# One turned tile for R, V and scaled A, and R loaded two tokens a partition, in a chunked RWKV-7 layer with a squared-ReLU feed-forward on one core

## The chip, the core and the metric

The kernel runs on one core of one Trainium2 chip. The metric is the device time of one execution in microseconds, lower is better. Before the change three runs took 263.15, 271.69 and 261.65 us, so the median is 263.15. One more execution, the profiled one, took 262.35 us with a span of 260.7 us between its first and its last instruction.

The engines that appear below: PE (TensorE, matmuls and transposes; PEld is its weight load), DVE (VectorE), ACT (ScalarE), POOL (GpSimd), and SP (SyncE), which only issues DMAs. Each works through its own instructions in their order and waits for others by semaphores.

## What is computed

Inputs are six tensors r, k, v, w, a, b of 4 batches x 8 heads x 768 tokens x 40, and two weights, 320 x 2048 and 2048 x 320. For every batch and head a 40 x 40 state runs over the tokens; then a feed-forward with a squared ReLU follows:

```python
for t in range(S):
    y[:, :, t] = np.einsum('bhd,bhde->bhe', rt, state)
    Sa = np.einsum('bhde,bhe->bhd', state, at)
    state_decay = state * wt[:, :, None, :] - np.einsum('bhd,bhe->bhde', Sa, bt)
    state = state_decay + np.einsum('bhd,bhe->bhde', vt, kt)
...
h = x @ w_in
r = np.maximum(h, 0.0)
g = r * r
return (g @ w_out).astype(np.float32)
```

Here x is y with the heads of a token side by side, 3072 x 320.

## The kernel before

The tokens are cut into 6 chunks of 128, so that there are 24 "batches" m (chunk m // 4, batch element m % 4), each with 8 heads, and 48 steps st (a half batch of four heads each). A batch goes through these stages; every stage has a short name, and the whole program is a list of such names.

- Loads on SP (`load`, line 85): lW, lK, lB, lA, lV, lR, each 128 tokens x 8 heads x 40 floats, 160 bytes a row. K and B share a tile, R and V share one. There are four buffers of each.
- The decay: ln takes the logarithm of w, cs sums it over the tokens by a matmul, xi and gp take exponentials (GI, GP), cx the difference between.
- Scaling and casting into padded tiles (each head's 40 columns padded to 64, so that two heads fill 128): pk makes K*GI and B*GI, pa makes A*GP (line 207), both into the padded tile KBA; cv casts R and V into the padded tile RV (lines 153, 155, 157 by engine).
- Turning (heads' dimensions onto the partitions). TensorE transposes into PSUM (`turned`, line 218) followed by an eviction: kt with kv for K and B in batches 0 to 19, ta with at for A and rm with rv for R and V in batches 0 to 7. DMA transposes on SP for the rest: ka (line 255) turns A from batch 8 on, and K, B and A together in the last four batches; rt (line 231) turns R and V from batch 8 on.
- a (st_a_mm, line 287) multiplies turned K and B with turned A for a step. av0 and av1 evict the two products with a mask on VectorE, or plainly on ScalarE, in which case POOL cuts them with aq0 and aq1. p, m, k1, c, k2, s, x (b_p, b_m, corr, b_c1, b_sn, b_x) solve for the step's corrections in PSUM.
- t and tv turn the corrections; e (st_ex_mm, line 410) multiplies turned R with turned V and with the corrections; ev0, ev1, eq0, eq1 evict and cut as before. z, kb, y, u (st_z, st_kb, st_y, st_u) make the output and the next state.
- xt and xv turn the output for the feed-forward; fr, fa, fb are its first matmuls, ra and rb the ReLU on ScalarE, q the square on POOL or VectorE (line 568), o1 and o2 the second matmuls, ov the eviction and ow the store.
- wt, wd and wo load the weights (POOL issues; wd, line 508, is a copy on SP of one piece of the first weight into the other half of the partitions, and waits for that piece). w are matmuls on ones that do nothing but keep TensorE busy. f and i fill tiles with constants. jk, en, ep, es and fl check a bound on the data, by which a general loop would replace the last steps.

What sets the order is the string ORDER: it lists all names with their batch or step, with the engine after a colon (`:P` POOL, `:D` VectorE, `:A` ScalarE) and the PSUM bank after `@`. The program is emitted in that order, and each engine, and SP with its DMAs, works in it. `pick` holds engine and bank of each name; whether a batch has, say, a `kt` at all is also read from it, as in b_ka.

The transposes that the change touches read as follows before it:

```python
def b_rt(m):
    o = bt[m]
    nc.sync.dma_start_transpose(
        out=o.RVT[:].rearrange("p u j t -> p (u j) t"),
        in_=o.RV[:].rearrange("p u h e -> p (u h e)"))
```

Of the kernel before, what the change touches and what calls it, by code (L numbers as in the profile page):

```python
# [18 lines left out]
def kernel(  # L19
# [62 lines left out]
    def load(key, m):  # L82
        pair, u = SHARED.get(key, (key, 0))
        c, bb = divmod(m, NB)
        nc.sync.dma_start(
            out=natural(pair, m)[:, u],
            in_=nat_srcs[key][bb, :, c * L:(c + 1) * L, :].rearrange("h t e -> t h e"))
# [8 lines left out]
    IDb = gl.tile([128, 128], BF16, name="IDb")  # L96
    MEX = gl.tile([128, 4, L], BF16, name="MEX")
# [10 lines left out]
    def fill(k):  # L108
# [7 lines left out]
        elif k < 16:  # L116
            key, i = (("KBA", k - 5) if k < 9 else ("G", k - 9) if k < 12 else ("RV", k - 12))
# [43 lines left out]
    def home(m):  # L161
        o = bt[m] = Batch()
        o.G, o.KB, o.RV = (pads[key][m % len(pads[key])] for key in ("G", "KBA", "RV"))
        o.RVT, o.YN = RVs[m % 4], YNs[m % 3]
# [41 lines left out]
    def b_pa(m):  # L206
        engine("pa", m).tensor_tensor(out=bt[m].KB[:, 2, :, 0:D], in0=nat.pop(("A", m))[:, 0],  # L207
                                      in1=bt[m].GP[:], op=ALU.mult)

    def b_cv(m):  # L210
        move(pick["cv", m][0], bt[m].RV[:, :, :, 0:D], nat.pop(("RV", m))[:])

    def turned(pad, us=(0, 1), t_=None, **place):
        if t_ is None:
            t_ = ps.tile([128, len(us), PB, L], BF16, name="tt", **place)
        for x, u in enumerate(us):
            for j in range(PB):
                nc.tensor.transpose(
                    out=t_[:, x, j, :], identity=IDb[:],
                    in_=pad[:, u, 2 * j:2 * j + 2, :].rearrange("p a b -> p (a b)"))  # L220
        return t_

    def b_rm(m):
        bt[m].t1 = turned(bt[m].RV, **bank("rm", m))

    def b_rv(m):
        move(pick["rv", m][0], bt[m].RVT[:], bt[m].t1[:])

    def b_rt(m):
        o = bt[m]  # L230
        nc.sync.dma_start_transpose(
            out=o.RVT[:].rearrange("p u j t -> p (u j) t"),
            in_=o.RV[:].rearrange("p u h e -> p (u h e)"))
# [4 lines left out]
    def kbt(m):  # L238
        o = bt[m]
        if not hasattr(o, "KBT"):  # L240
            o.KBT = chp.tile([128, 3, PB, L], BF16, name="KBT", tag="KBT", bufs=4)
        return o.KBT

    def b_kv(m):
        move(pick["kv", m][0], kbt(m)[:, 0:2], bt[m].t2[:])

    def b_ta(m):
        bt[m].t3 = turned(bt[m].KB, us=(2,), **bank("ta", m))

    def b_at(m):  # L250
        move(pick["at", m][0], kbt(m)[:, 2], bt[m].t3[:, 0])

    def b_ka(m):
        o, lo = bt[m], 2 if ("kt", m) in pick else 0
        nc.sync.dma_start_transpose(
            out=kbt(m)[:, lo:3].rearrange("p u j t -> p (u j) t"),
            in_=o.KB[:, lo:3].rearrange("p u h e -> p (u h e)"))
# [22 lines left out]
    def st_a_mm(st):  # L280
# [3 lines left out]
        for u in range(2):  # L284
            for i in range(2):
                for s in range(2):
                    nc.tensor.matmul(out=ca[s][:, i, u, :], lhsT=o.KBT[half(s), u, j0 + i, :],  # L287
                                     rhs=o.KBT[half(s), 2, j0 + i, :], start=(i == 0 and u == 0),
# [32 lines left out]
    def b_p(m):  # L321
# [3 lines left out]
        if c > 0:  # L325
            for j in range(PB):
                nc.tensor.matmul(out=P[:, j, :, 0:D], lhsT=o.KBT[:, 2, j, :],
# [292 lines left out]
    def get_flag():  # L620
# [4 lines left out]
        f.0:D lW.0 f.1:P w.1@f f.14:D f.5:P w.16@0 lW.1 i.1 w.8@s lK.0 w.4@f f.3:D i.0 ln.0 f.2:P  # L625
        f.6:P cs.0@s w.7@f w.2@1 cx.0 ln.1 f.10:P lB.0 cs.1@u xi.0 lA.0 f.20:D w.0@f gp.0 pk.0:D
        kt.0@0 lK.1 xi.1 lB.1 f.8:P f.11:D f.16:P w.14@f pa.0:P ta.0@f at.0:A w.15@s cx.1 w.3@x
        gp.1 lW.2 i.2 f.4:P lA.1 lW.3 kv.0:D a.0@0e a.1@xf lV.0 pk.1:D ln.2 av0.0:D pa.1:D f.15:P
        av1.1:A w.11@f av0.1:A av1.0:A lR.0 cs.2@u f.12:P lV.1 cx.2 ta.1@f kt.1@1 w.13@e xi.2
        aq0.0 at.1:D kv.1:D lR.1 a.2@x1 gp.2 av0.2:D av1.2:D aq1.2 a.3@fu lK.2 w.10@0 aq0.2 aq1.1  # L630
        aq0.1 lB.2 cv.0:A aq1.0 ln.3 av0.3:D f.19:P f.18:P p.0@e m.0:A cs.3@0 lK.3 k1.0 jk.0 xi.3
        av1.3:D w.9@x cv.1:A lA.2 rm.0@u c.0 lB.3 aq0.3 cx.3 aq1.3 f.9:P k2.0 p.1@f lA.3 gw.0:P
        gw.2:D gw.1:P s.0:A t.0@f rv.0:D gc.0@s lW.4 tv.0:D f.7:P m.1:A w.12@e f.17:P pk.2:D k1.1
        lV.2 f.13:P wt.1 e.1@0f ev1.1:D pa.2:P ev0.1:D jk.1 rm.1@x pk.3:P gp.3 lW.5 kt.2@e eq0.1
        rv.1:A ta.2@f lR.2 at.2:A lV.3 kv.2:D e.0@u1 ev0.0:A eq0.0 c.1 eq1.1 a.4@ex k2.1 gw.3:D
        av0.4:A z.1@0 ev1.0:D eq1.0 pa.3:P x.0 gl.0 s.1:A kt.3@u aq0.4 cv.2:P lR.3 kb.1 z.0@s
        av1.4:D kb.0 t.1@f gl.1 u.0 y.0 ta.3@x at.3:D kv.3:A ln.4 tv.1:A a.5@ef av0.5:D av1.5:A
        wt.2 u.1 aq1.4 e.3@s1 ev1.3:A lA.4 aq1.5 ev0.3:A y.1 a.6@fx av0.6:D ln.5 eq1.3 a.7@ef
        av1.6:A cs.4@1 av1.7:D eq0.3 e.2@uf cx.4 aq0.5 lK.4 av0.7:D gp.4 aq0.6 ev0.2:D cs.5@f
        ev1.2:D z.3@u p.2@0 xt.0@x pa.4:P xi.5 rm.2@e aq1.6 wt.4 m.2:A z.2@f lB.4 k1.2 wt.3 aq0.7  # L640
        eq0.2 xi.4 lK.5 eq1.2 c.2 kb.2 wt.9 k2.2 rv.2:A cx.5 cv.3:A ta.4@e lB.5 aq1.7 kb.3 wd.0
        p.3@1 lA.5 wt.0 u.2 y.2 s.2:A at.4:D y.3 wt.7 pk.4:D xv.0:A m.3:A t.2@f rm.3@f tv.2:D k1.3
# [275 lines left out]
```

## Time and profile before

| | |
|---|---|
| three runs, us | 263.15, 271.69, 261.65 |
| profiled execution, us | 262.35 |
| its span, us | 260.7 |
| busy PE | 243.1 (93%) |
| busy DVE | 204.7 (79%) |
| busy ACT | 205.7 (79%) |
| busy POOL | 207.9 (80%) |
| DMA packets, MB | 184470, 38.48 |
| packets under 512 bytes | 180064 |

The page gives the busy time of each engine, its share of the span and the costliest groups of instructions. A group's row has the line, the engine and the operation, what is written and read, the count, the busy time and the mean in nanoseconds, and then how long the engine was idle just before these instructions and what ended that. Matmuls overlap, so that the mean of one (about 220 ns for a transpose) is longer than the distance between two. SP's instructions are DMA issues; a duration of such a row contains waiting for a place in the queue. A window's row has its length, the busy time and count of PE, PEld, DVE, ACT and POOL, then the clock granted to TensorE, the mean busy share of the 16 DMA engines, and GB/s.

### The profile page before, as it was taken

To read this page: it belongs to the slowest core of one execution; us is meant where nothing else is said; L and a number is where in the kernel's file an instruction comes from. 1 tells how busy PE (TensorE), PEld (TensorE's weight loads), DVE (VectorE), ACT (ScalarE), POOL (GpSimd) and SP (SyncE) were. 2 spreads that over 40 slices of the span, in tenths; PEclk is the share of its full clock that TensorE was granted. 3 is DMA by queue.
4 is the path that set the end of the run, shared out by engine and by line. 5 is a ranking of instruction groups with operands and counts; after the bars stand their busy time and mean duration, and the time that the engine had idled before them with its cause. 6 is when DMAs were issued, how large, how long until landed. Compare 5 with 4: busy or idle time off the path is not lost.

```text
span 260.7 us, 9854 instructions
## 1 busy us (share of the span) xinstructions
PE 243.1 (93%) x4020; PEld 201.9 (77%) x4020; DVE 204.7 (79%) x421; ACT 205.7 (79%) x470; POOL 207.9 (80%) x238
## 2 busy tenths in 40 slices
PE   8987887999999999999999988999799998999993
PEld 7876676988788877778868777788778886888872
DVE  2789986899899997989787957787889979965240
ACT  3688995999798888878978878898789777678830
POOL 5597998599998574989698996899889468968640
PEclk9999997999999999999999999999999999999998
DMA  7999998999988999989989999999899985022011
GB/s 125 153 178 167 158 191 159 182 155 173 181 144 143 148 165 170 179 168 181 177 148 177 157 174 172 177 158 192 162 160 189 175 146 101 28 69 78 28 55 60
DMA packets 184470, 38.48 MB, mean 148 GB/s; under 512 B 180064, under 2 KB 183136, under 8 KB 184416
## 3 DMA queue, kind: packets, MB, share of 16 engines
q1 hardware_dynamic: 183072, 35.14, 78.8%
q0 software_dynamic: 1344, 2.62, 6.2%
q8 instruction: 33, 0.54, 0.9%
q14 instruction: 21, 0.17, 0.2%
HBM read 28.84 MB, written 3.93 MB: 126 GB/s over the span
## 4 chain that ended last, share of the span: by engine, by line
PE 24%; POOL 13%; DMA 5%; issue 3%; ACT 2%; DVE 2%; SPq 1%; POOLq 0%; DVEq 0%; ACTq 0%
PE hp L542 7%; DMA NW<-in_w_dram 3%; POOL Gt L568 3%; POOL EX L307 2%; POOL KBAp L202 2%; DMA KBT<-KBAp 2%; POOL x L360 2%; POOL KBAp L207 2%; POOL Cc L361 1%; PE ca L287 1%; PE ex L410 1%; PE P L344 1%; PE uy L456 1%; ACT hs L562 1%; PE op__6251 L577 1%
## 5 line engine op out<-in xcount | busy, mean ns | idle before, releaser
L542 PE MATMUL hp<-XS,WIN 128*128 128x256 bf16 (+3 forms) x720 | 73.1, 255 | 2.4 <-DMA WIN<-in_moe_w_in_dram 1.5
L562 ACT ACTIVATE hs<-hp 128x512 bf16<-128x512 f32 x96 | 55.1, 599 | 15.0 <-PE hp L542 9.4
L542 PEld LDWEIGHTS <-WIN 128*128 128x128 bf16 (+1 forms) x720 | 49.9, 115 | 9.6 <-issue 6.3
L568 POOL TENSOR_TENSOR Gt<-hs 128x1024 bf16<-128x1024 bf16 x24 | 45.9, 1914 | 8.7 <-ACT hs L562 6.2
L302 DVE TENSOR_TENSOR CN<-ca,MEX 128x512 bf16<-128x512 f32 x63 | 41.5, 683 | 7.6 <-PE ca L287 6.9
L577 PEld LDWEIGHTS <-Gt 128*128 128x128 bf16 x384 | 35.6, 98 | 13.2 <-issue 0.9
L302 DVE TENSOR_TENSOR EX<-ex,MEX 128x512 bf16<-128x512 f32 x58 | 38.1, 682 | 1.9 <-PE ex L410 0.9
L307 POOL TENSOR_SCALAR_AFFINE_SELECT EX<-EX 128x512 bf16<-128x512 bf16 x38 | 28.0, 744 | 7.6 <-ACT EX L300 7.1
L307 POOL TENSOR_SCALAR_AFFINE_SELECT CN<-CN 128x512 bf16<-128x512 bf16 x33 | 22.2, 677 | 10.6 <-ACT CN L300 8.4
L300 ACT ACTIVATE EX<-ex 128x512 bf16<-128x512 f32 x38 | 22.0, 599 | 5.7 <-PE ex L410 5.6
L207 POOL TENSOR_TENSOR KBAp<-NA,GP 128x320 bf16<-128x320 f32 x18 | 16.6, 922 | 11.6 <-DMA NA<-in_a_dram 5.7
L365 ACT ACTIVATE jk<-CN 128x1024 bf16<-128x1024 bf16 x24 | 25.4, 1057 | 0.0
L202 POOL TENSOR_TENSOR KBAp<-NKB,GI 128x640 bf16<-128x640 f32 x14 | 22.0, 1572 | 1.3 <-PE ca L287 0.7
L300 ACT ACTIVATE CN<-ca 128x512 bf16<-128x512 f32 x33 | 19.5, 603 | 4.3 <-PE ca L287 4.0
L361 POOL TENSOR_TENSOR Cc<-x,SN 128x320 bf16<-128x320 f32 x24 | 20.3, 846 | 1.9
L456 PE MATMUL uy<-KBAp,EX 128*128 128x40 bf16 x384 | 21.7, 181 | 0.0
L568 DVE TENSOR_TENSOR Gt<-hs 128x1024 bf16<-128x1024 bf16 x24 | 21.4, 897 | 0.2
L360 POOL TENSOR_TENSOR x<-Mc,c 128x320 f32<-128x320 bf16 x24 | 19.9, 829 | 0.2
L287 PE MATMUL ca<-KBT 64*128 64x128 bf16 x384 | 18.1, 217 | 1.6 <-ACT KBT L153 0.6
L173 PE MATMUL cs<-lnW,UTI 128*128 128x320 f32 x48 | 19.1, 481 | 0.3 <-ACT CN L300 0.2
L456 PEld LDWEIGHTS <-EX 128*128 128x128 bf16 x384 | 18.4, 97 | 1.3 <-issue 0.7
L344 PEld LDWEIGHTS <-CN 128*128 128x128 bf16 x384 | 15.0, 96 | 4.8 <-issue 3.0
(150 smaller groups left out, 624.4 us busy)
## 6 DMA issues: line engine op xcount, KB each, us to landing
NW<-in_w_dram SPq DMA_DIRECT2D x24, 160.0 KB, 3.8
NKB<-in_k_dram SPq DMA_DIRECT2D x24, 160.0 KB, 3.8
NKB<-in_b_dram SPq DMA_DIRECT2D x24, 160.0 KB, 3.8
NA<-in_a_dram SPq DMA_DIRECT2D x24, 160.0 KB, 4.0
NRV<-in_v_dram SPq DMA_DIRECT2D x24, 160.0 KB, 3.8
NRV<-in_r_dram SPq DMA_DIRECT2D x24, 160.0 KB, 3.9
out_dram<-osb SPq DMA_DIRECT2D x24, 160.0 KB, 3.0
WOUT<-in_moe_w_out_dram POOLq DMA_DIRECT2D x2, 640.0 KB, 7.2
```

Source lines behind the costliest of these rows:

```text
L202: engine("pk", m).tensor_tensor(out=bt[m].KB[:, 0:2, :, 0:D], in0=nat.pop(("KB", m))[:], op=ALU.mult, in1=bt[m].GI[:].rearrange("p (u h) e ...
L300: nc.scalar.activation(out=out, in_=in_[:], func=ACTF.Copy)
L302: nc.vector.tensor_tensor(out=out, in0=in_[:], op=ALU.mult, in1=MEX[:].rearrange("p (i u) x -> p i u x", u=2))
L307: nc.gpsimd.affine_select(out=t_, in_=t_, pattern=[[0, 2], [0, 2], [1, L]], compare_op=ALU.is_gt, fill=0.0, base=0, channel_multiplier=-1)
L360: nc.gpsimd.tensor_tensor(out=t_[:], in0=part(Mc, m), in1=c1s.pop(m)[:], op=ALU.add)
L361: nc.gpsimd.tensor_tensor(out=part(Cc, m), in0=t_[:], in1=flat(SNs[m % NSN]), op=ALU.subtract)
L365: nc.scalar.activation(out=jk[:], in_=CNs[m, "b"][:].rearrange("p x i s u t -> p (x i s) u t")[:, :, 1, :], func=ACTF.Square, accum_out=AC ...
L456: nc.tensor.matmul(out=uy[:, (2 * i + s) * D:(2 * i + s + 1) * D], lhsT=EXs[st][:, i, s, u, :], rhs=o.KB[:, u, 2 * (j0 + i) + s, 0:D], sta ...
L542: nc.tensor.matmul(out=o.hp[u][:, i], lhsT=inner(g, rows, j), rhs=XSs[o.c][rows, g, o.bs, :], start=(o.begun[u] == 1), stop=(o.begun[u] > ...
L562: nc.scalar.activation(out=o.hs[:, u], func=ACTF.Relu, in_=o.hp[u][:].rearrange("p j a b -> p (j a b)"))
L568: engine("q", n).tensor_tensor(out=o.Gt[:, o.j0:o.j0 + 2 * o.per].rearrange("p j a b -> p (j a b)"), in0=hs, in1=hs, op=ALU.mult)
L577: nc.tensor.matmul(out=ops[n][:], rhs=WOUT[:, j, :], lhsT=Gts[h][:, b_, j, :] if h in SPLIT else Gts[h][:, j, b_, :], start=(j == 0), stop ...
```

## The change

The padded tile KBA becomes KB, and RV becomes RVA: scaled A is written behind R and V. The turned tiles move likewise (KBT has two parts, RVT three), and st_a_mm and b_p read turned A there. From batch 8 on, rt turns R, V and A with one DMA; ka is left for the last four batches alone, where it turns K and B. So there are 16 rt and 4 ka where there were 16 and 16.

In batches 0 to 7 R is loaded "paired": two DMAs of 64 partitions each, one for heads 0 to 3 and one for heads 4 to 7; a partition holds two neighbouring tokens, which lie side by side in memory, 320 bytes. A new name cr casts R from that layout, cv casts V alone there. turn_pairs turns R with four transposes whose results are laid into PSUM so that the even tokens come first; V is turned with a second identity IDp that sorts the tokens in the same way; rv then stores both with a stride of two, which puts the tokens back in their order. Turned A of these batches goes through ta and at as before, into the new place.

The whole of ORDER is new: order, engines and banks. The counts of the names are the same but for cr (8, new), ka (4 for 16) and i (4 for 3, IDp). Of engines: 130 of the masked evictions av and ev are on VectorE for 121 before; pk has 17 on POOL for 14; q has 22 on POOL for 24; gw has 18 on POOL for 16; tv has 18 on VectorE for 21, kv 11 for 13, rv 1 for 3; ov 7 for 10, m 11 for 8, pa 7 for 6, s 9 for 8, xv 13 for 12. Of the 21 fills 10 are on POOL for 16. fl stands before the last three w's instead of behind them.

The diff without ORDER, cut to its core:

```diff
     def load(key, m):
...
+        src, dst = nat_srcs[key][bb, :, c * L:(c + 1) * L, :], natural(pair, m)[:, u]
+        if key == "R" and paired(m):
+            for s in range(2):
+                nc.sync.dma_start(
+                    out=dst[half(s)].rearrange("p (h a) e -> p h (a e)", a=2),
+                    in_=src[PB * s:PB * s + PB].rearrange("h (p a) e -> p h (a e)", a=2))
+        else:
+            nc.sync.dma_start(out=dst, in_=src.rearrange("h t e -> t h e"))
+
+    def paired(m):
+        return ("cr", m) in pick
...
-            for key, n in (("KBA", 4), ("G", 3), ("RV", 4))}
-    RVs = [gl.tile([128, 2, PB, L], BF16, name=f"RV{i}") for i in range(4)]
+            for key, n in (("KB", 4), ("G", 3), ("RVA", 4))}
+    RVs = [gl.tile([128, 3, PB, L], BF16, name=f"RV{i}") for i in range(4)]
...
-            (MEX, MEX, [[0, 4], [1, L]], ALU.is_gt))[k]
+            (MEX, MEX, [[0, 4], [1, L]], ALU.is_gt),
+            (IDp, ones_b, [[1, 2], [2, 64]], ALU.is_equal))[k]
...
-        engine("pa", m).tensor_tensor(out=bt[m].KB[:, 2, :, 0:D], in0=nat.pop(("A", m))[:, 0],
+        engine("pa", m).tensor_tensor(out=bt[m].RV[:, 2, :, 0:D], in0=nat.pop(("A", m))[:, 0],
...
     def b_cv(m):
-        move(pick["cv", m][0], bt[m].RV[:, :, :, 0:D], nat.pop(("RV", m))[:])
+        lo = 1 if paired(m) else 0
+        move(pick["cv", m][0], bt[m].RV[:, lo:2, :, 0:D], nat["RV", m][:, lo:2])
+
+    def b_cr(m):
+        move(pick["cr", m][0], bt[m].RV[:, 0, :, 0:D].rearrange("p (a h) e -> p a h e", a=2),
+             nat["RV", m][:, 0].rearrange("p (h a) e -> p a h e", a=2))
...
+    def turn_pairs(pad, t_):
+        by = t_[:, 0].rearrange("p (s j) (a t) -> p j a s t", s=2, a=2)
+        at = pad[:, 0].rearrange("p (a j x) e -> p j a (x e)", a=2, j=2)
+        for j in range(2):
+            for a_ in range(2):
+                nc.tensor.transpose(out=by[:, j, a_], in_=at[:, j, a_], identity=IDb[:])
...
     def b_rv(m):
-        move(pick["rv", m][0], bt[m].RVT[:], bt[m].t1[:])
+        n = 2 if ("rm", m) in pick else 1
+        to, at = bt[m].RVT[:, 0:n], bt[m].t1[:]
+        if paired(m):
+            to = to.rearrange("p u j (t a) -> p (u j) a t", a=2)
+            at = at.rearrange("p u j (a t) -> p (u j) a t", a=2)
+        move(pick["rv", m][0], to, at)
...
     def b_rt(m):
-        o = bt[m]
+        o, lo = bt[m], 2 if ("rm", m) in pick else 1 if ("rn", m) in pick else 0
+        hi = 2 if ("ta", m) in pick else 3
         nc.sync.dma_start_transpose(
-            out=o.RVT[:].rearrange("p u j t -> p (u j) t"),
-            in_=o.RV[:].rearrange("p u h e -> p (u h e)"))
+            out=o.RVT[:, lo:hi].rearrange("p u j t -> p (u j) t"),
+            in_=o.RV[:, lo:hi].rearrange("p u h e -> p (u h e)"))
...
     def b_ka(m):
-        o, lo = bt[m], 2 if ("kt", m) in pick else 0
         nc.sync.dma_start_transpose(
-            out=kbt(m)[:, lo:3].rearrange("p u j t -> p (u j) t"),
-            in_=o.KB[:, lo:3].rearrange("p u h e -> p (u h e)"))
+            out=kbt(m)[:].rearrange("p u j t -> p (u j) t"),
+            in_=bt[m].KB[:].rearrange("p u h e -> p (u h e)"))
...
-                                     rhs=o.KBT[half(s), 2, j0 + i, :], start=(i == 0 and u == 0),
+                                     rhs=o.RVT[half(s), 2, j0 + i, :], start=(i == 0 and u == 0),
```

Of ORDER, the stretch from pa.12 to a.24 after the change, to which the prediction refers:

```
pa.12:P gl.10 en.13 y.19 fr.15@ue ln.13 e.20@10 u.47 jk.11 x.10 fa.15 gw.11:P k1.11 xt.9@x
kt.12@f ev0.20:A c.11 ra.15 xv.9:D lK.14 fb.15 k2.11 ev1.20:A kv.12:D rt.12 ow.4 s.11:A
rb.15 q.13:D o2.5 a.24@u0
```

and the weight loads with the copies on SP in the order of each program, before and after:

```
wt.1 wt.2 wt.4 wt.3 wt.9 wd.0 wt.0 wt.7 wd.1 wt.5 wt.6 wt.8
wt.1 wt.2 wd.0 wt.7 wt.3 wt.0 wt.4 wt.9 wd.1 wt.5 wt.6 wt.8
```

More of the change, by code (lines that the diff above doesn't have):

```diff
@@ L218, in turned, with b_rn @@
                 nc.tensor.transpose(
[L219 removed]
+                    out=t_[:, x, j, :], identity=(by or IDb)[:],
                     in_=pad[:, u, 2 * j:2 * j + 2, :].rearrange("p a b -> p (a b)"))
         return t_
+    def turn_pairs(pad, t_):
[4 more added lines that the diff above has]
+                nc.tensor.transpose(out=by[:, j, a_], in_=at[:, j, a_], identity=IDb[:])
+    def b_rn(m, us=()):
+        o = bt[m]
+        o.t1 = ps.tile([128, 1 + len(us), PB, L], BF16, name="tt", **bank("rm" if us else "rn", m))
+        if paired(m):
+            turn_pairs(o.RV, o.t1)
+            if us:
+                turned(o.RV, us=us, t_=o.t1[:, 1:], by=IDp)
+        else:
+            turned(o.RV, us=(0, *us), t_=o.t1)
     def b_rm(m):
[L224 removed]
+        b_rn(m, us=(1,))
     def b_rv(m):
[L227 removed]
+        n = 2 if ("rm", m) in pick else 1
+        to, at = bt[m].RVT[:, 0:n], bt[m].t1[:]
+        if paired(m):
+            to = to.rearrange("p u j (t a) -> p (u j) a t", a=2)
+            at = at.rearrange("p u j (a t) -> p (u j) a t", a=2)
+        move(pick["rv", m][0], to, at)
     def b_rt(m):
[L230 removed]
+        o, lo = bt[m], 2 if ("rm", m) in pick else 1 if ("rn", m) in pick else 0
+        hi = 2 if ("ta", m) in pick else 3
         nc.sync.dma_start_transpose(
[L232 to L233 removed]
+            out=o.RVT[:, lo:hi].rearrange("p u j t -> p (u j) t"),
+            in_=o.RV[:, lo:hi].rearrange("p u h e -> p (u h e)"))
     def b_kt(m):
@@ L630 @@
[L630 to L641, printed above, removed]
```

295 lines of the change are left out of this document (151 added, 144 removed).

## The prediction

> **What bounds the kernel now.** First the windows (busy time by engine and stretch; the last columns are the granted clock, the DMA share and GB/s), then who waited for whom.
>
> ```profile
> span 260.7 us, 9854 instructions
> 0.00:40.00 40.00, 34.24 (x580) 28.36 (x580) 31.41 (x64) 31.33 (x70) 32.01 (x59) 1.00 0.98 163
> 40.00:60.00 20.00, 19.47 (x394) 17.55 (x394) 16.26 (x37) 16.64 (x40) 16.23 (x18) 0.91 0.94 161
> 60.00:240.00 180.00, 173.22 (x2858) 143.22 (x2855) 152.29 (x311) 148.44 (x342) 151.45 (x159) 1.00 0.91 154
> 240.00:261.00 21.00, 16.13 (x194) 12.77 (x192) 4.78 (x12) 9.27 (x21) 8.20 (x5) 0.95 0.13 44
> ```
>
> TensorE (first number after the comma) is the bound from 40 us on: 173.2 of 180 us in the long middle, while VectorE, ScalarE and POOL have 15 to 18% to spare. Its idle time is 5.8 us before 40, 0.5 to 60, 6.8 in the middle and 4.9 at the end. So a change that leaves its matmuls alone can win at most the first three, 13.1 us, and lose without limit by new waits. The DMA share near 1 says that loads leave little room either.
>
> Three places show what TensorE and its suppliers wait for: the group of st_a_mm, the waits of the SP queue, and two pieces of SP's timeline.
>
> ```profile
> L287 PE MATMUL ca<-KBT 64*128 64x128 bf16 x384 | 18.1, 217 | 1.6 <-ACT KBT L153 0.6 <-DMA KBT<-KBAp 0.5 <-DVE KBT L157 0.3
> PEld L287 <- DMA KBT<-KBAp: 1.1, 3, 0.6
> 200.53 4.29 DMA KBT<-KBAp
> SPq L508 <- DMA WIN<-in_moe_w_in_dram: 6.9, 1, 6.9
> 33.18 0.81 SPq L85 DMA_DIRECT2D NA<-in_a_dram  x1
> 41.00 0.47 SPq L508 DMA_DIRECT2D WIN<-WIN  x1
> ```
>
> The transfer that turns A ends last for st_a_mm in four places (0.5 and three in 1.1, together 1.6 us), and one of them stands in the chain that ended last. And from 33.99 to 41.00 SP issues nothing: it waits for a weight piece with all later loads behind it.
>
> **The matmuls.** A paired batch turns R with four transposes and V with four, as now; t, kt and ta keep their counts.
>
> ```profile
> L218 PE MATMUL tt<-IDb,KBAp 128*128 128x128 bf16 x192 | 15.0, 219 | 1.7 <-POOL KBAp L207 1.0 <-ACT jm L376 0.5 <-DVE KBAp L202 0.2
> L218 PE MATMUL tt<-IDb,RVp 128*128 128x128 bf16 x64 | 4.9, 219 | 0.0
> ```
>
> After it they are still 192 + 64 = 256, 32 of them with another identity. I take 0.
>
> **The merged transfer, batches 8 to 23.** Twelve short transposes (A alone, 4 blocks of 128x128) go, sixteen grow from 8 blocks to 12 and now carry A, and four shrink from 12 to 8. Blocks in all: 12*4 + 4*12 + 16*8 = 224 before, 16*12 + 4*8 = 224 after. Nothing is saved in DMA work; SP saves issues. The rows: A alone (x12) with its landings, K, B and A together (x4) with theirs, R and V (x16) with theirs; landings count from the issue's start.
>
> ```profile
> L255 SPq DMA_TRANSPOSE KBT<-KBAp x12: 1194/1290/2260, 72.7 to 183.7; - x12
> DMA to landing us min/median/max: 2.4/3.0/4.9
> L255 SPq DMA_TRANSPOSE KBT<-KBAp x4: 1447/1712/2335, 191.6 to 216.1; - x4
> DMA to landing us min/median/max: 3.7/4.2/4.7
> L231 SPq DMA_TRANSPOSE RV<-RVp x16: 1261/1552/2418, 83.1 to 230.3; - x16
> DMA to landing us min/median/max: 3.1/3.8/5.7
> ```
>
> SP saves 12*1.29 = 15.5 us of issue and pays 16*(1.71 - 1.55) = 2.6 back. In front of that stands a longer way for A: 4.2 us where it had 3.0, and it starts only when V, R and A are all cast. Behind a waiting transpose SP holds the loads of the next batches; they are taken up a batch or more later, so I price those at 0, and if that cover is gone they fall under the second rival.
>
> What is late next is st_a_mm of the batch. Between the later of cv and pa and the first `a` of the batch, ORDER puts a certain amount of TensorE's work. For batch 12 it is fr.15, e.20, fa.15, k1.11, xt.9, kt.12, fb.15, k2.11 and o2.5, which by pieces of the chain
>
> ```profile
> 170.13 0.22 PE hp L542 x4
> 164.77 0.33 PE ex L410 x8
> 171.89 0.44 PE hp L542 x4
> 166.71 0.20 PE P L344 x8
> 167.25 0.17 PE xt L489 x3
> 171.44 0.45 PE tt L218 x8
> 162.58 1.09 PE op__4234 L577 x8
> L207 POOL TENSOR_TENSOR KBAp<-NA,GP 128x320 bf16<-128x320 f32 x18 | 16.6, 922 | 11.6 <-DMA NA<-in_a_dram 5.7 <-ACT GP L189 3.9 <-ACT jk L365 1.8
> ```
>
> is 0.22 + 0.33 + 0.44 + 0.20 + 0.17 + 0.45 + 0.44 + 0.20 + 1.09 = 3.5 us. The same count, an estimate from such pieces, gives for batches 8 to 23: 4.6, 4.9, 6.2, 4.9, 3.5, 5.3, 6.9, 4.2, 4.9, 8.3, 7.6, 6.5, 8.2, 9.1, 5.5, 5.4 (in the old order, from pa to `a`, 3.7 to 11.3). Needed are the product on POOL (0.92) and the landing: 0.92 + 4.2 = 5.1 us. Six batches fall short, by 0.5, 0.2, 0.2, 1.6, 0.9 and 0.2: 3.6 us, against 1.6 now, so +2.0. Bounds: -1.6 if no `a` waits any more; and with the longest landing seen for A, 4.9, the need is 5.8, nine batches fall short, and their shortfalls add up to 9.0, so +7.4. I take +2.0, by the four rows that have the same 12 blocks.
>
> **R by pairs, batches 0 to 7.** 1024 packets of 160 bytes become 512 of 320, in two issues.
>
> ```profile
> q1 hardware_dynamic: 183072, 35.14, 78.8%
> L85 SPq DMA_DIRECT2D NRV<-in_r_dram x24: 572/764/2436, 9.9 to 204.1; - x24
>   DMA NRV<-in_r_dram: 3.2, 3
> ```
>
> A packet of this queue takes 0.788*260.7*16/183072 = 17.9 ns of one engine; 8*512 = 4096 fewer are at most 4096*17.9/16 = 4.6 us of DMA time, and nothing if the time goes by bytes. The eight extra issues cost SP up to 8*0.764 = 6.1 us. Whoever casts R or V waited for them 3.2 us in three places only, so neither end is on the path directly: I take 0, with -4.6 and +6.1 as ends. The Trainium skill, page "DMA: Bandwidth & Descriptors", section "Why small descriptors are slow (HBM only)", gives each packet a fixed three cycles on top of one per 32 bytes; by that, as an estimate, 320 bytes cost 13 cycles where two of 160 cost 16, so 3/16 of R's DMA time goes and not half of it, and the sum would be at most 1.7 us lower.
>
> Casting V and R apart (cv, cr) makes two half casts of one, and the eviction rv stores with a stride.
>
> ```profile
> L153 ACT ACTIVATE RVp<-NRV 128x640 bf16<-128x640 f32 x10 | 7.4, 744 | 2.0 <-DMA NRV<-in_r_dram 2.0
> L153 ACT ACTIVATE SN<-P 128x320 bf16<-128x320 f32 x16 | 7.1, 444 | 1.7 <-PE P L344 1.7
> L153 ACT ACTIVATE RV<-tt 128x1024 bf16<-128x1024 bf16 x5 | 5.1, 1025 | 0.1
> ```
>
> Two halves are 0.89 for 0.74, +1.2 us over eight batches and three engines. The strided store is in no row; seven of eight are on ScalarE, where I take today's 1.025 (ends: 0, and +1.0 each if it halves the rate). With the third identity on POOL I put +0.3 on the path of the start, where the engines work 78% of the time.
>
> **The order anew.** The start: the weight piece for which SP stood still is now the third that POOL issues and was the seventh. The seven microseconds shrink to little, but TensorE was not idle all that time (5.8 us before 40, much of it earlier): I take -1.0, ends -6.9 and 0. Evictions and products change engines:
>
> ```profile
> L302 DVE TENSOR_TENSOR CN<-ca,MEX 128x512 bf16<-128x512 f32 x63 | 41.5, 683 | 7.6 <-PE ca L287 6.9 <-ACT jk L365 0.4
> L300 ACT ACTIVATE CN<-ca 128x512 bf16<-128x512 f32 x33 | 19.5, 603 | 4.3 <-PE ca L287 4.0
> L307 POOL TENSOR_SCALAR_AFFINE_SELECT CN<-CN 128x512 bf16<-128x512 bf16 x33 | 22.2, 677 | 10.6 <-ACT CN L300 8.4 <-PE hp L542 2.0
> L568 POOL TENSOR_TENSOR Gt<-hs 128x1024 bf16<-128x1024 bf16 x24 | 45.9, 1914 | 8.7 <-ACT hs L562 6.2 <-DVE Gt L568 2.4
> L568 DVE TENSOR_TENSOR Gt<-hs 128x1024 bf16<-128x1024 bf16 x24 | 21.4, 897 | 0.2
> ```
>
> Nine masked evictions go from ScalarE with POOL's cut to VectorE (+6.1; -5.4 and -6.1), two squarings from POOL to VectorE (+1.8, -3.8). Three products pk go from VectorE to POOL, and seven turned tiles (tv, kv, rv) from VectorE to ScalarE, which gives back about as much. The sums stay within some 4 us of 205 to 208 and their spare share of 15 to 18% hides them: 0. At the end the last four squarings are all on VectorE (three on POOL now); TensorE runs on there with other work, so -0.3, ends -1.0 (one 1.914 against 0.897) and 0. What else the new order does can't be read off; its bounds are those of the idle time above.
>
> **The sum.** The profiled execution took 262.35 us, 1.65 more than its span and 0.8 less than the median of 263.15. 262.35 + 2.0 + 0.3 - 1.0 - 0.3 = 263.35, so 263.4.
>
> **The rivals.**
> Slower: A comes late. If the merged transfer lands 4.9 us or more after its issue in the tight batches, st_a_mm becomes the stop of the in-order TensorE in nine batches: 262.35 + 7.4 + 0.3 - 0.3 = 269.7. It decides once the shortfalls exceed some 7 us. For it: four places where A's shorter transfer already ends last, and a DMA share near 1. Against: after each such stop the other engines are ahead, and the next shortfall shrinks.
> Faster: the line at SP was the hidden bound. 15.5 us of issue less and the stop at 33.99 gone let loads come early enough that half of the 13.1 us of idle before 240 goes: 262.35 - 6.5 - 0.3 + 0.3 = 255.9, call it 256. For it: SP's loads queue behind waiting transposes. Against: casters waited little for R and V.
> The pairs give nothing back: if the packets' time goes by bytes and the second issue delays each load behind it while the start hangs on loads, the first four batches pay 4*0.764 = 3.1 and the gain of 1.0 is lost: 263.4 + 4.1 = 267.5. The Trainium skill, same page, section "Rules for kernel authors", says that two transfers to separate halves of the partitions run one after the other and advises one transfer; by that rule this case holds.
>
> **How the numbers follow.** Forecast (263.4) 0.30; pairs lost (267.5) 0.06; slower (269.7) 0.36; faster (256) 0.28. Two per cent, about what a measurement of this kernel can tell from no change, is 5.3 us: 257.9 and 268.4. So faster 0.28, within 0.36, slower 0.36. The range takes both rivals in, 255.5 to 271.0; the forecast's own is 260.5 to 266.5 (start -1.0 to 0, A's wait -1.6 to +3).
>
> **What would show it.** A's step: waits of L287 for the transfer into RV (not KBT) of 3 to 4 us in all, landings near 4.2 us; over 9 us is the slower rival. SP: no stop over 2 us at the weight twin before 45 us, and transposes near 1.7 us each. Pairs: R's landing of a half under 3.8 us. Engines: VectorE, ScalarE and POOL each within 5 us of now. The faster rival shows as TensorE idle under 4 us before 60. I am wrong if TensorE's idle time grows where no transfer into RV ends last: then the new order did it.

## The result and the profile after

In 12 runs each, the changed kernel took 259.79 us in the median (258.38 to 264.1), the kernel before 262.18 (260.63 to 271.69): ratio 0.9907, interval 0.9881 to 0.9934. A second measurement of the same changed kernel (e1_again below) gave 0.9922. So it is faster by some 0.8 to 0.9%, 2 us; 263.4, a little slower, was forecast. The profiled execution of the changed kernel took 264.1 us, 262.4 of them the span: it is a disturbed run, with TensorE three times at half clock, and the ratio leaves such runs out.

The windows of that execution, with the columns of those shown for the kernel before (time and count of TensorE, its weight loads, VectorE, ScalarE and POOL; then granted clock, DMA share, GB/s):

```profile
span 262.4 us, 9826 instructions
0.00:40.00 40.00, 33.19 (x560) 28.21 (x560) 29.98 (x68) 31.55 (x70) 31.14 (x56) 0.96 0.95 164
40.00:60.00 20.00, 18.69 (x391) 16.04 (x386) 18.69 (x40) 18.13 (x40) 16.43 (x19) 1.00 1.00 163
60.00:240.00 180.00, 174.07 (x2857) 144.13 (x2858) 153.81 (x307) 148.95 (x341) 150.43 (x154) 0.98 0.86 153
240.00:263.00 23.00, 18.34 (x227) 14.60 (x223) 7.63 (x20) 10.10 (x21) 0.89 (x2) 1.00 0.14 48
```

TensorE's idle time is now 6.8 us before 40 (it was 5.8), 1.3 to 60 (0.5) and 5.9 in the middle (6.8). The start has become worse, the middle better. The groups, the transfers and the queue that answer to the rows of the prediction:

```profile
L324 PE MATMUL ca<-RV,KBT 64*128 64x128 bf16 x384 | 16.8, 218 | 0.6 <-ACT KBT L163 0.5
q1 hardware_dynamic: 178720, 35.14, 75.2%
L269 SPq DMA_TRANSPOSE RV<-RVAp x16: 1313/1570/2685, 73.6 to 219.7; - x16
DMA to landing us min/median/max: 3.7/3.9/5.6
L88 SPq DMA_DIRECT2D NRV<-in_r_dram x16: 606/622/2017, 10.0 to 60.8; - x16
DMA to landing us min/median/max: 2.5/4.0/7.9
```

First line: st_a_mm no longer waits for any transfer; the places in which A's transpose ended last are gone, and no wait for the merged transfer has come in their place. (The prediction counted four such places with 1.6 us. There were three: the stop at 102.4 us stands in both of its rows, as 0.5 us of the matmuls and as 0.6 of their weight loads.) The transposes of 12 blocks cost SP 1.57 us, the price of those of 8 (1.55), and land after 3.9.

Fixed windows mix the start with the middle, so from here on I cut each execution by its own work: from the first matmul of step 16 of st_a_mm (a step of batch 8, the first batch with transposes by DMA) to that of step 46. The middle row of each fence is that stretch. Kernel before, then e1_again, the changed kernel:

```profile
0.00:78.30 78.30, 71.56 (x1284) 60.60 (x1286) 65.00 (x135) 63.82 (x146) 66.20 (x93) 0.98 0.98 164
78.30:222.00 143.70, 137.37 (x2268) 113.44 (x2266) 122.07 (x249) 119.29 (x276) 118.88 (x126) 1.00 0.98 164
```

```profile
0.00:85.70 85.70, 74.31 (x1292) 62.89 (x1294) 68.04 (x143) 67.87 (x150) 63.80 (x92) 0.94 0.90 154
85.70:225.50 139.80, 137.29 (x2307) 113.81 (x2303) 122.44 (x252) 117.54 (x269) 122.38 (x125) 1.00 0.97 170
```

The middle went from 143.7 to 139.8 us with the same TensorE work (137.4 and 137.3): its idle time fell from 6.3 to 2.5 us. The start went from 78.3 to 85.7, of which a part is the clock (0.94). So the change wins about 4 us in the middle and gives part of it back before. One execution can mislead, but the middle holds: cut in the same way, it takes 139.5 to 142.6 us in every kept execution below that has the merged transfer and no added loads (142.6 in the first one, with one of its stretches at half clock). Which part of the change does which is the question of the experiments.

### The profile page after: what moved, and what is told of

The parts are those of the page before. It is cut to its first block, busy times and chain, and to the rows that moved or that the text cites. A ratio compares the mean times of both kernels' runs of the same rounds, so it can differ in the third digit from the quotient of the medians.

```text
span 262.4 us, 9826 instructions
## 1 busy us (share of the span) xinstructions
PE 244.3 (93%) x4020; PEld 203.0 (77%) x4020; DVE 210.1 (80%) x432; ACT 208.7 (80%) x469; POOL 198.9 (76%) x228
## 4 chain that ended last, share of the span: by engine, by line
PE 64%; DVE 9%; SPq 9%; DMA 7%; ACT 4%; issue 3%; POOL 2%; DVEq 0%; POOLq 0%; ACTq 0%
PE hp L579 18%; SPq L92 6%; PE cs L183 4%; PE ca L324 3%; PE ex L447 3%; PE tt L233 3%; PE P L381 3%; DVE Gt L605 2%; DMA WIN<-in_moe_w_in_dram 2%; PE uy L493 2%; DMA NW<-in_w_dram 2%; PE tb L425 2%; SPq L269 2%; SPq L88 2%; PE uy L488 1%
## 5 line engine op out<-in xcount | busy, mean ns | idle before, releaser
L605 POOL TENSOR_TENSOR Gt<-hs 128x1024 bf16<-128x1024 bf16 x22 | 42.0, 1913 | 3.8 <-ACT hs L599 3.3
L339 DVE TENSOR_TENSOR EX<-ex,MEX 128x512 bf16<-128x512 f32 x64 | 42.0, 681 | 3.1 <-PE ex L447 2.7
L344 POOL TENSOR_SCALAR_AFFINE_SELECT EX<-EX 128x512 bf16<-128x512 bf16 x32 | 21.3, 674 | 11.3 <-ACT EX L337 8.3
L212 POOL TENSOR_TENSOR KBp<-NKB,GI 128x640 bf16<-128x640 f32 x17 | 26.8, 1577 | 3.0 <-DMA NKB<-in_b_dram 1.6
L605 DVE TENSOR_TENSOR Gt<-hs 128x1024 bf16<-128x1024 bf16 x26 | 24.4, 943 | 2.3 <-ACT hs L599 2.3
L337 ACT ACTIVATE EX<-ex 128x512 bf16<-128x512 f32 x32 | 18.7, 604 | 6.7 <-PE ex L447 6.7
L493 PE MATMUL uy<-KBp,EX 128*128 128x40 bf16 x384 | 21.6, 181 | 0.5 <-POOL EX L344 0.5
L208 POOL TENSOR_TENSOR Gp<-NW,GP 32x320 bf16<-32x320 f32 x18 | 17.2, 958 | 4.1 <-issue 2.8
L217 POOL TENSOR_TENSOR RVAp<-NA,GP 128x320 bf16<-128x320 f32 x17 | 15.6, 919 | 6.2 <-ACT GP L199 3.1
L509 DVE TENSOR_TENSOR YN<-uy,GP 128x160 bf16<-128x160 f32 (+1 forms) x48 | 16.3, 347 | 4.4 <-PE uy L493 3.9
```

The source lines that it names most:

```text
L212: engine("pk", m).tensor_tensor(out=bt[m].KB[:, 0:2, :, 0:D], in0=nat.pop(("KB", m))[:], op=ALU.mult, in1=bt[m].GI[:].rearrange("p (u h) e ...
L337: nc.scalar.activation(out=out, in_=in_[:], func=ACTF.Copy)
L339: nc.vector.tensor_tensor(out=out, in0=in_[:], op=ALU.mult, in1=MEX[:].rearrange("p (i u) x -> p i u x", u=2))
L344: nc.gpsimd.affine_select(out=t_, in_=t_, pattern=[[0, 2], [0, 2], [1, L]], compare_op=ALU.is_gt, fill=0.0, base=0, channel_multiplier=-1)
L493: nc.tensor.matmul(out=uy[:, (2 * i + s) * D:(2 * i + s + 1) * D], lhsT=EXs[st][:, i, s, u, :], rhs=o.KB[:, u, 2 * (j0 + i) + s, 0:D], sta ...
L605: engine("q", n).tensor_tensor(out=o.Gt[:, o.j0:o.j0 + 2 * o.per].rearrange("p j a b -> p (j a b)"), in0=hs, in1=hs, op=ALU.mult)
```

## The experiments

The theory after the result: SP's line of issues was on the path, and the merged transfer won by taking twelve issues out of it (20 transposes for 32); the prediction had put that line at nothing. Rivals: the new order did it, not the transfer; or the DMA queues did, which have one transpose less a batch. All ratios are to the kernel before, taken on the same chip (its medians there: 264.3 to 265.9 us). e1 to e4 ran on one chip, e5 to e8, e9 to e12 and e13 to e18 on three others; between these groups it is two such ratios that are compared.

**e1_again**, no edit.

> The changed kernel as it is. Both theories: about 259.5 us, 0.988 to 0.993 of before; its trace is to show where TensorE's idle time shrank: theory 'parts' (the merged transfer, the pairs or the earlier weight piece bring it) expects the gain before 60 us or in the waits for turned A and for loads; theory 'order' (the new order of everything else brings it) expects it spread over the middle and the end, with waits on engines.

0.9922 (0.9891 to 0.9954). It is the base for what follows.

**e2_split**: the merged transfer is taken apart, all else stays; tr.8 to tr.23 stand in ORDER just ahead of rt.8 to rt.23. SP issues 36 transposes now, four more than before the change, since ka turned K, B and A of the last four batches together there.

```
+    def b_tr(m):
+        nc.sync.dma_start_transpose(
+            out=bt[m].RVT[:, 2:3].rearrange("p u j t -> p (u j) t"),
+            in_=bt[m].RV[:, 2:3].rearrange("p u h e -> p (u h e)"))
...
-        hi = 2 if ("ta", m) in pick else 3
+        hi = 2
```

> As changed, but from batch 8 on turned A has its own DMA again, issued just ahead of the one for R and V (for K and B in the last four it stays apart). 16 more issues on SP, same blocks. If the merge brought the gain by SP's issues (16 x 1.3 = 21 us more on SP), 2 us or more slower, about 262. Rival, that A's late landing cost something: A lands 1 us earlier, up to 2 us faster. Theory 'order': within 0.5 us of the changed kernel.

1.0106 (1.0049 to 1.0162): taking the transfer apart costs 1.8%, give or take 0.6 by the two intervals, and more than undoes the change. Its windows, cut in the same way:

```profile
0.00:82.40 82.40, 71.45 (x1294) 59.86 (x1296) 67.53 (x143) 67.22 (x151) 65.33 (x92) 1.00 0.94 162
82.40:230.50 148.10, 140.94 (x2305) 115.61 (x2300) 123.38 (x252) 117.86 (x269) 120.73 (x125) 0.98 0.90 160
```

The middle is 148.1 us where e1 had 139.8. Of these 8.3 us 3.6 are TensorE's own busy time (140.9 for 137.3), in an execution that has it at half clock twice there, for 3.4 us each; the rest is idle time. The DMA share speaks against the rival of the queues: 0.90 of 148.1 is 133 us of DMA time, 0.97 of 139.8 in e1 is 136. By that the transfers have no more work than in e1, and the engines that carry them stand idle longer.

One place shows how the line delays a transfer. K and B of batch 21 are scaled on POOL, SP issues A's transposes of batches 20 and 21, then the transpose of that K and B, and TensorE waits for it:

```profile
196.29 1.54 POOL L212 TENSOR_TENSOR KBp<-NKB,GI 128x640 bf16<-128x640 f32 x1
197.37 1.20 SPq L274 DMA_TRANSPOSE RV<-RVAp  x1
201.53 2.21 SPq L274 DMA_TRANSPOSE RV<-RVAp  x1
206.09 1.28 SPq L297 DMA_TRANSPOSE KBT<-KBp  x1
PE ca L329 <- DMA KBT<-KBp: 2.9, 1, 2.9
```

The product is ready at 197.83, and its transpose goes out 8.3 us later; SP issues one transfer after the other all that time. In e1 the same transpose goes out 4.0 us after its product, and TensorE doesn't wait for it. For A's own transposes TensorE waits nowhere in e2: what the added issues delay is what stands behind them.

**e3_unpaired** and, on another chip, **e15_unpaired_again**: the merged transfer stays, R of batches 0 to 7 is loaded in one transfer as V is, without pairs and without the strided store.

```
-        if key == "R" and paired(m):
+        if False:
...
-             nat["RV", m][:, 0].rearrange("p (h a) e -> p a h e", a=2))
+             nat["RV", m][:, 0])
```

> As changed, but R of batches 0 to 7 is loaded like V in one DMA with 160 bytes a row; the two casts stay apart, all transposes use the plain identity, and the eviction stores without a stride. If pairs win by packets, up to 4.6 us slower, about 261 to 264; if the second issue costs more than the packets give, 1 to 4 us faster; theory 'order': within 0.5 us.

> The kernel of e3_unpaired again, beside e14_halves_again on the same chip: 0.983 to 0.989 if pairs are a loss by themselves; 0.990 or above if the first figure was chance.

0.9856 (0.9823 to 0.989) and 0.983 (0.9768 to 0.9892). Without pairs the kernel is faster by another 0.7% (give or take 0.5) on the chip of e1_again, and beats both. The middle of e15 is that of e1, that of e3 is 141.8 us:

```profile
0.00:81.70 81.70, 72.49 (x1292) 61.60 (x1294) 68.12 (x143) 65.86 (x151) 64.30 (x92) 0.96 0.96 162
81.70:222.00 140.30, 137.32 (x2306) 113.54 (x2301) 122.56 (x252) 117.45 (x269) 121.38 (x125) 1.00 0.99 170
```

**e8_order_only**: both edits, split and unpaired; what is left of the change is the order (with casts apart), and there are 36 transposes where the kernel before has 32.

> The new order with neither part: A turned by its own DMA just ahead of R and V, R loaded like V (casts apart as changed). If the parts add up, 1.0106 x 0.9856 / 0.9922 = 1.004 of before, so that the merge has brought all of the gain and the rest of the order nothing. If the new order itself is better, below 0.995.

1.0098 (1.006 to 1.0135). The new order, with four transposes more, loses 1%. From here to e3 only the merging differs, by sixteen issues (twelve of them are what the change saves): 1.0098 to 0.9856, 2.4% (give or take 0.5) or 6.4 us. With that the rival of the order falls.

**e7_halves** and **e14_halves_again**: e3, but R of batches 0 to 7 comes in two loads of 64 partitions.

```
+            for s in range(2):
+                nc.sync.dma_start(out=dst[half(s)], in_=src[:, half(s)].rearrange("h t e -> t h e"))
```

> As the unpaired kernel (0.986 of before), but R of batches 0 to 7 in two DMAs of 64 partitions, with 160 bytes a row as ever: eight more issues, the same packets, no stride anywhere. If the second issue is what the pairs cost, back to the changed kernel's 0.992; if it is the strided eviction, it stays at 0.986.

> The kernel of e7_halves again, whose interval was missing: R of the first eight batches not paired, but loaded in two halves of 64 partitions. Unpaired in one load was 0.9856, paired 0.9922. If the second issue is what pairs cost, 0.990 to 0.994; if it is the strided store of the turned tile, 0.984 to 0.988.

The first took 264.17 us in the median beside 264.75 for the kernel before and has no interval; inconclusive. The second: 0.9813 (0.9753 to 0.9874), on the chip where e15 had 0.983. The second issue costs nothing that can be seen. What the pairs lose lies in the pairs themselves: their loads, their turns or the strided store. For the store there are rows, e3 first, then e1_again (ns: shortest, median, longest; seven of the ten are 128x1024):

```profile
L163 ACT ACTIVATE RV<-tt x10: 597/1023/1052, 10.0 to 67.5; 128x1024 bf16<-128x1024 bf16 x7, 128x512 bf16<-128x512 bf16 x3
```

```profile
L163 ACT ACTIVATE RV<-tt x10: 597/1322/1379, 9.3 to 73.5; 128x1024 bf16<-128x1024 bf16 x7, 128x512 bf16<-128x512 bf16 x3
L167 DVE COPY RV<-tt x6: 415/420/1306, 19.5 to 84.9; 128x512 bf16<-128x512 bf16 x5, 128x1024 bf16<-128x1024 bf16 x1
```

The strided store takes 1.32 us on ScalarE instead of 1.02, and 1.31 on VectorE where e15's took 0.68: 7*0.30 + 0.62 = 2.7 us of engine time. That it is the whole 0.7% (1.7 us) was not tried apart.

**e4_late_weight**: the weight pieces in their old order, in the changed kernel.

```
-wt.7
+wt.4
...
-wt.0
+wt.9
...
-wt.4
+wt.0
...
-wt.9
+wt.7
```

> As changed, but with the weight loads on POOL in the old order, so that the piece that SP's copy waits for is the seventh again. SP should stand still for some 5 us between 30 and 45 us. If that stop was what the change removed, 1 to 2.4 us slower; if TensorE does not hang on those loads, within 0.5 us.

0.9898 (0.9862 to 0.9934), no loss, though SP stands still again:

```profile
SPq L545 <- DMA WIN<-in_moe_w_in_dram: 5.3, 1, 5.3
```

That stop, the most visible wait of SP before, costs nothing that the interval shows.

**e5_dummy**: is it the issue, or what is issued? Two loads of half a KB, which nobody reads, are issued by SP ahead of each transpose.

```
+    def b_dm(m):
+        for i in range(2):
+            nc.sync.dma_start(out=DUM[0:16, 2 * m + i, :], in_=w[0, 0, 0:16, 0:8])
```

> As changed (one transfer for R, V and A), with two tiny loads (16 partitions x 32 bytes, read by nobody) on SP just ahead of each rt of batches 8 to 23: 32 more issues, about 32 x 0.5 = 16 us of SP time and next to no DMA work. Theory 'line at SP' (what the merge saves is SP's issue time): 1 to 2% slower than the changed kernel, like the split one (1.011 of before). Rival 'transposes' (a second DMA transpose costs by itself, or R and V land later): within 0.5% of the changed kernel.

1.021 (1.0157 to 1.0263), 2.9% above e1: more than the split. In its profile: the loads (ns: shortest, median, longest), the transposes, then who waited for transfers in the middle (us, times, longest), and the window of the middle:

```profile
L277 SPq DMA_DIRECT2D DUM<-in_w_dram x32: 410/572/2068, 73.5 to 224.3; - x32
```

```profile
L269 SPq DMA_TRANSPOSE RV<-RVAp x16: 1278/1444/2658, 74.8 to 224.9; - x16
DMA to landing us min/median/max: 3.7/3.8/5.4
```

```profile
PE ca L330 <- DMA RV<-RVAp: 6.4, 11, 1.6
POOL KBp L212 <- DMA NKB<-in_b_dram: 4.0, 3, 3.4
```

```profile
79.60:229.10 149.50, 139.09 (x2305) 113.84 (x2300) 120.36 (x252) 118.02 (x271) 121.70 (x126) 1.00 0.91 160
```

Two issues of 0.57 us put each transpose off by more than a microsecond: in e1 it goes out 0.1 us (median) after the last cast of its batch, in e5 1.3. The transposes themselves are as short as in e1 and land as fast, but TensorE now waits for them in 11 places, 6.4 us in all. From the issue of a batch's transpose to its first matmul of st_a_mm lie 4.8 to 8.9 us in e1, median 5.7, read from the trace for the 16 batches; in e5 3.8 to 5.7, median 4.4, against landings of 3.7 to 5.4. So the merged transfer has a microsecond or more in hand in twelve of the 16 batches of e1 (median 1.7), and what stands ahead of it in SP's line uses that up. The DMA queues are no rival here either: 0.91 of 149.5 is 136 us, as in e1.

**e9_old_tiny**: the same loads in the kernel before.

> The kernel before, with two loads of 16 rows of 32 bytes issued by SyncE just ahead of each of the sixteen transposes of R and V. Theory (SyncE's issue line is what the middle of the kernel hangs on, in the old order too, where it is taken 129.7 of the 140 us from 60 to 200): 32 more issues of some 0.6 us find no free place, and the kernel gets slower by as much as the changed one did from the same loads (2.9%), ratio 1.02 to 1.03. Rival (only the new order has its loads so late that SyncE's line shows): ratio 1.00 to 1.01.

1.0418 (1.036 to 1.0476), more than either theory had. SP's line was on the path in the old order too, with less in hand. Waits for transfers in its middle, of the kernel before and then of e9:

```profile
DVE KBAp L207 <- DMA NA<-in_a_dram: 1.6, 1, 1.6
POOL KBAp L207 <- DMA NA<-in_a_dram: 0.8, 1, 0.8
ACT lnW L168 <- DMA NW<-in_w_dram: 0.9, 1, 0.9
PE ca L287 <- DMA KBT<-KBAp: 0.5, 1, 0.5
PE ex L410 <- DMA RV<-RVp: 0.3, 1, 0.3
```

```profile
PE ca L293 <- DMA KBT<-KBAp: 7.2, 6, 1.9
POOL KBAp L207 <- DMA NA<-in_a_dram: 4.3, 2, 3.4
ACT lnW L168 <- DMA NW<-in_w_dram: 3.2, 3, 1.4
PE ex L416 <- DMA RV<-RVp: 2.2, 2, 1.5
```

The loads stood ahead of R's and V's transposes, but the longest waits are for A's (7.2 us for 0.5), and A and w themselves are waited for longer as well (4.3 for 2.4, 3.2 for 0.9): what stands behind in the line is late.

**e10_old_out_act** and **e6_out_on_act**: the other way round, a shorter line. The 24 output stores are issued by ScalarE, in the kernel before and in the changed one.

```
-        nc.sync.dma_start(out=out[tok:tok + L, :], in_=osbs[n][:])
+        nc.scalar.dma_start(out=out[tok:tok + L, :], in_=osbs[n][:])
```

> The kernel before, with its 24 output stores issued from ScalarE's queue. SyncE is relieved of 24 issues and of its waits for finished outputs, about what the merged transfer takes off it. Theory (SyncE's issue line): faster by 1 to 2%, ratio 0.98 to 0.99, though ScalarE pays 24 issues. Rival (it is the transposes themselves, one DMA job less a batch, that help): 1.00 or above.

> As changed, but the 24 output stores are issued from ScalarE's queue and not from SP: some 24 x 0.6 = 14 us less on SP, which also no longer waits for the evictions. Theory 'line at SP': faster by 0.3 to 1%, if ScalarE does not lose more by issuing. Rival: the merge has taken all that SP's line had to give, so no change, or slower by ScalarE's 24 issues.

0.9908 (0.9867 to 0.9949) before, as much as the whole change brings; 0.9892 (0.9831 to 0.9954) in the changed kernel, nothing that the intervals tell from e1's 0.9922. After the merging a shorter line brings no more gain that can be seen. In e10 the middle is 141.3 us, between the two kernels (a DMA share above 1 says that packets' times overlap, so that such shares are a rough measure):

```profile
79.00:220.30 141.30, 136.49 (x2270) 113.36 (x2266) 120.61 (x248) 119.44 (x276) 119.45 (x126) 1.00 1.01 167
```

**e11_tiny_act**, **e13_split_act**, **e16_split_out_act**, **e17_tiny_out_act**: four tries to keep the added transfers and give SP its time back, through ScalarE's queue: the tiny loads, or the transpose of A, issued by ScalarE (nc.scalar in the place of nc.sync), or the output stores, in e2 and in e5.

> The changed kernel with the same 32 tiny loads as in e5_dummy, but issued by ScalarE. Theory (SyncE's line): the loss of 2.9% goes; what stays is 32 issues on ScalarE, ratio to before 0.99 to 1.00. Rival (the tiny loads hurt in the DMA queues, whoever issues them): 1.015 or above, as in e5_dummy.

> The changed kernel with A turned by its own transpose as in e2_split, but that transpose is issued from ScalarE's queue. The DMA queues do the same work as in e2_split (ratio to before 1.0106), SyncE's line is as short as in the changed kernel (0.992). Theory (SyncE's issue line is what counts): near the changed kernel, 0.99 to 1.002, the upper part if 16 issues of 1.2 us on ScalarE, and its waits behind the product of A, cost something there. Rival (a second DMA transpose a batch costs in the DMA queues): 1.008 to 1.013 as in e2_split.

> e2_split (A turned by its own transpose on SyncE, 1.0106) with the 24 output stores issued from ScalarE, which in the changed kernel itself moved nothing (0.9892 against 0.9922). All DMA work of the split stays, but SyncE's line is as short as in the changed kernel. Theory (SyncE's line): back to 0.990 to 0.999. Rival (DMA work of the second transpose): 1.007 to 1.013.

> e5_dummy (32 tiny loads on SyncE, 1.021) with the 24 output stores issued from ScalarE. Theory (SyncE's line): most of the loss goes, 0.995 to 1.005, since SyncE has 8 issues more than the changed kernel. Rival (tiny loads cost in the DMA queues, as e11_tiny_act's 1.0076 allows): 1.01 to 1.02.

1.0076 (1.0015 to 1.0138), 1.1677 (1.1621 to 1.1733), 1.0137 (1.0092 to 1.0181) and 1.0168 (1.0087 to 1.0249). Only the first went the theory's way, and only by half; whether the other half is ScalarE's 32 issues or the loads themselves, these runs don't tell. In e13 neither theory holds: pieces of the chain that ended last show why.

```profile
143.37 3.08 DMA RV<-RVAp
146.55 4.65 DMA RV<-RVAp
```

The transpose of SP's queue is issued at 143.37 and lands 3.08 us later; only then, at 146.55, does ScalarE's begin. The two queues take turns, with ScalarE and SP standing still meanwhile. The program makes them do so: ahead of ScalarE's transpose stands a wait for the semaphore that SP's transpose sets when it has landed. (The Trainium skill, page "DMA: Bandwidth & Descriptors", section "Rules for kernel authors", asks for that: transposes from two queues have to be one after another. The trace agrees that they are; no run here shows what happens without the wait.) In e17 it is output stores that wait, in ScalarE's part of the timeline:

```profile
142.46 0.34 ACTq L631 DMA_DIRECT2D out_dram<-osb  x1
142.90 0.60 ACT L605 ACTIVATE hs<-hp 128x512 bf16<-128x512 f32 x1 [3.54 <-DMA RV<-RVAp]
178.56 0.40 ACTq L631 DMA_DIRECT2D out_dram<-osb  x1
179.00 0.44 ACT L189 ACTIVATE GI<-cs 128x320 f32<-128x320 f32 x1 [3.30 <-DMA NRV<-in_v_dram]
```

SP's transpose was issued at 136.10 and landed 6.34 us later, at 142.44; the first store goes at 142.46, and ScalarE's next eviction has stood behind it for 3.54 us. The second store waits in the same way for a load of V, issued by SP at 174.46 and landed at 178.48. Neither store needs what it waits for. The trace shows why: all transfers of SP and ScalarE share eight completion semaphores, which the program hands out in turn, and each issue waits until the transfer that had its semaphore last has landed. Four stores are held up by that in e17, 8.6 us in all, four in e16, 3.3 us, and one in e6, 0.9 us; in e1, e2 and e5 no issue of SP stands idle for it by more than 0.3 us. Who TensorE waited for in e17:

```profile
PE tb L431 <- ACT SN L163: 3.1, 2, 2.4
PE ex L453 <- ACT hs L605: 3.0, 1, 3.0
```

It hardly waits for a transpose any more (0.5 us), as SP's theory wants, but for ScalarE. So e16 and e17 came out where the rival of the DMA queues had put them, and by another way than it says. In e17 the stores' waits (8.6 us, and 6.1 us in TensorE's two rows) are enough for the 6.5 us that it lies above e1; in e16 they (3.3 us) are less than its 5.7, and the same stores cost nothing that shows in e6. How the 1.8 to 2.4% of the merging divide between SP's issue time and whatever else a second transpose costs stays open. For the issue speak e5 and e9, where no transpose was added, the late transpose of batch 21 in e2, and e2's DMA time, which did not grow.

**e12_unp_pk** and **e18_unp_out_act**: can the faster version be bettered? e3 with the products of batches 8 and 9 changed between VectorE and POOL (pk.8:P, pk.9:D); e3 with the output stores on ScalarE.

> The faster version, changed kernel with R of the first eight batches loaded in one transfer, and with the products of K and B of batch 8 on POOL and of batch 9 on VectorE (they were the other way round). In the unpaired kernel TensorE waited 1.5 us at 72 to 78 us for the product of batch 8, whose turn on VectorE came late. If that knot is a cost of its own: 0.978 to 0.983. If another wait takes its place: 0.985 as without it.

> The faster version (e3_unpaired 0.9856, e15_unpaired_again 0.983) with the 24 output stores issued from ScalarE. If SyncE's line still costs something there: 0.975 to 0.981. If what is left lies elsewhere, as it did in e6_out_on_act: 0.982 to 0.987.

0.9854 (0.9792 to 0.9916) and 0.9825 (0.9769 to 0.9881): no difference from e3 and e15 beyond the intervals of 0.6%. The knot at 72 to 78 us was no cost of its own that shows, and neither is what is left of SP's line.

## Why the prediction was wrong

It summed four small terms to +1.0 us; measured is -2. By its steps:

- **Matmuls, 0**: right. 160 + 3*32 = 256 of them are in the groups of tt, and TensorE's work in the middle is the same to 0.1 us.
- **The merged transfer, +2.0**: the step that failed, in both its halves. "What is late next is st_a_mm": in e1 one wait of 0.4 us for the transfer, none in the first profile, where the shortfalls had been put at 3.6 us in six batches. (The 1.6 us set against them were 1.1, since one stop was counted twice; the term would have been +2.5.) I had set the landing against an estimate of TensorE's work between pa and `a`; in the run the transpose goes out 4.8 us or more before `a` and lands in 3.9 to 4.0 (median of the first profile and of e1). And "Behind a waiting transpose SP holds the loads of the next batches ... I price those at 0": that cover was not there. e8 against e3 shows the merging at -2.4%, -6.4 us; e5 and e9 show that a microsecond more ahead of a transpose costs 2.9 and 4.2%. The saving of 15.5 us of issue that I had worked out and then left without a price is, as far as e5, e9 and the late transpose in e2 show, where the gain came from. A line whose issues fill 129.7 of the 140 us from 60 to 200 had no cover to give (not all of that is the bare issue: one and the same load takes SP 0.37 to 3.2 us there): I had looked for who waits for loads, and found little, but not for what stands in line ahead of each transpose.
- **Pairs, 0**: some +0.7%, +1.7 us, by e3 against e1. Within the ends, and the second issue, which made the upper one, is not it: e14 has it and loses nothing. The rival that built on it falls, and the rule of the Trainium skill that stood beside it (page "DMA: Bandwidth & Descriptors", section "Rules for kernel authors": two halves of the partitions run one after the other) shows in no time here. The lower end was empty: R's packets fell, and q1's time with them, but TensorE never waited for R's load, and the others waited for it as long as before, 3.2 us, in four places. R's half landed after 4.0 us (median) and not under 3.8.
- **Casts apart, strided store, +0.3**: the store was in no row and I took today's 1.025; it is 1.32 on ScalarE, 1.31 on VectorE. Too low by up to 2.7 us of engine time, a part of the pairs' loss.
- **The order, -1.0**: not borne out. The weight block brings 0 (e4). "What else the new order does can't be read off": with four transposes more it costs about 1%, 2.6 us (e8), of which by proportion, as an estimate, 4/16 of the merging's 6.4, or 1.6, go to those four. The start is where it shows: in executions with a granted clock of 1.00 up to step 16, that takes 78.6 and 79.0 us in the old order (e9, e10), 80.7 and 82.0 in the new one without pairs (e3, e7).
- **Engines and tail**: ScalarE stays within 5 us of before; VectorE does in e1 (204.7 to 208.5), and just not in the first profile (210.1); POOL, 207.9 to 198.9, does not. The end, from step 46 on, went from 38.7 to 37.6 us (222.0 to the span's 260.7, and 225.5 to 263.1): -1 for the -0.3.

The faster rival had the mechanism, SP's line, but priced it by TensorE's idle time before 240 and looked for its sign before 60. It came in the middle, and two losses of the same change, order and pairs, hid two thirds of it: 2.6 - 6.4 + 1.7 = -2.1 us (e8, e8 to e3, e3 to e1, by 264.9 us). That this gives the change is no proof, since the steps lead from the kernel before to e1; and with the four transposes moved, as an estimate, it is 1.0 - 4.8 + 1.7. The stated range, 255.5 to 271.0, took in both rivals, so that 259.8 lies inside it says nothing for any of them.

## What to carry to other kernels

A queue that is busy nearly all the time is a resource like an engine: price an issue that is saved or added by what stands behind it in line, and test that with a few issues that do nothing. When a change of several parts moves little, build it without each part: here the best kernel is the change without its pairs. Relief for a queue is worth something only until the line has room; after that the same edit brings nothing that shows. And an issue that moves to another engine can stop that engine, if it has to wait there for a semaphore that it shares with other transfers.

## What was not expected of the hardware

A bf16 copy out of PSUM that stores with a stride of two elements took 1.32 us for 1.02 on ScalarE, and 1.31 for 0.68 on VectorE (there one copy in each run). And a stop of TensorE of 2.9 us was followed by 3.4 us at half clock: in e2 TensorE stood from 207.4 to 210.3, in the wait for batch 21, and the granted clock is 0.5 from 211.1 to 214.5, which shows in the window

```profile
200.00:220.00 20.00, 17.00 (x256) 13.84 (x253) 14.24 (x29) 13.21 (x29) 14.14 (x14) 0.91 1.04 165
```

as 0.91 over 20 us. By that, as an estimate, this wait cost another 3.4/2 = 1.7 us of work at half speed. What decides it isn't shown: a stop of 1.8 us was followed by 3.4 us at half clock in e2 (from 144.0) and in e8 (from 143.2), and by none in e3 (from 141.3).
